# Storing the last dwq and dwo blocks from GpSimd's queue, two partitions and then 126

## The chip, the cores and the metric

The kernel runs on one core of one Trainium2 chip. The metric is device time of one execution in microseconds; the median of several runs is compared. Beside it there is one profiled execution, whose page and trace are quoted below. In the trace, times count from the span's start; "SPq" and "POOLq" are the instruction queues of SyncE and GpSimd, and DMA queue q1 carries what SyncE issues, q0 what GpSimd issues.

## The reference

Forward and backward pass of a gated mix of two branches, for one token (batch 1, sequence 1, D = 640), with ten outputs: the result and nine gradients.

```python
x = A_x
g = _sigmoid((x * gate_w).sum(-1, keepdims=True))
a = _A_ref(x, A_k_cache, A_v_cache, A_wq, A_wo)   # q = x@wq; softmax(q k^T) v; @wo; 32 heads, 4096 keys, Dh 128
b = _B_ref(x, B_w1, B_b1, B_w2)                   # mish(x@w1 + b1) @ w2; F = 1728
return g * a + (1 - g) * b
...
_out, _vjp = jax.vjp(_f, A_x, A_k_cache, A_v_cache, A_wq, A_wo, B_w1, B_b1, B_w2, gate_w)
_grads = _vjp(grad_out)
```

All arrays are bf16. The K and V caches are 32 MB each, and so are their gradients. The gradients of wq (640 x 4096) and wo (4096 x 640) are outer products: dwq is x times the gradient of q, dwo is the attention output o times the gradient that comes in.

## The kernel before

The loop runs over the 32 heads `h`, in 8 groups `g` of 4. For each head it loads K and V (1 MB each, `load_k`, `load_v`), transposes them on TensorE, forms the softmax and its gradient, and builds the gradients of K and V as outer products on VectorE (`dk_out`, `dv_out`, through `out_half`, L598), each stored with one transfer of 1 MB from SyncE's queue (L616). All heavy loads and stores are issued by SyncE, in the order in which they are written out by hand in the loop; an issue waits on SyncE until its data are ready, and holds up the issues behind it.

The weights come in blocks. A tile `wq_p` (128 partitions x 5 x 1024 bf16, 1.25 MB) holds wq of two groups; a tile `wo_g` (128 x 4 x 640 bf16, 640 KB) holds wo of one. When a group is done, `f_dwq` and `f_dwo` write the gradients over the weights in the same tiles, and `f_dwq_st` (L377) and `f_dwo_st` (L386) store them. In DRAM, a partition's piece of dwq is five runs of 2048 bytes that lie far apart; its piece of dwo is one run of 5120 bytes.

After the loop stands a tail for the last head and the last group. In it the gradient of the last K block is stored (L616), then come dwq (`f_dwq` on VectorE, `l_dwq` on ScalarE for the last head) with its store, dwo (`l_dwo` on VectorE, L383) with its store, and a short chain that ends in `fin_rows`, 15 rows of 256 bytes, which GpSimd stores in three transfers of five rows (L920 to L922). GpSimd's queue is otherwise hardly used: it has memsets at the start, a few small transfers and two multiplications; between L802 and L920 it stands waiting.

```python
    dk_out(h, 1)
    ...
    for c in range(RC):
        l_dwq(c, 3, 4)
    f_dwq_st(g)
    for t in range(G):
        l_dwo(t)
    f_dwo_st(g)
    l_add(g, NG, True)
```

Of the kernel before, what the change touches and what calls it, by code (L numbers as in the profile page):

```python
# [16 lines left out]
def kernel(  # L17
# [24 lines left out]
    nc = tc.nc  # L42
    P = 128
    _, H, Sk, Dh = A_k_cache.shape
    D = A_x.shape[-1]
# [4 lines left out]
    G = 4  # L50
    NG = H // G
    GD = G * Dh
# [17 lines left out]
    dwq_v = out_4.rearrange("(rc r) c -> r rc c", r=P)  # L70
    wo4_v = A_wo.rearrange("(g p t) n -> g p t n", p=P, t=4)
    dwo4_v = out_5.rearrange("(g p t) n -> g p t n", p=P, t=4)
# [29 lines left out]
    kts, vts, wqs, wos = {}, {}, {}, {}  # L102
# [11 lines left out]
    wqp = {}  # L114
# [255 lines left out]
    def f_dwq(g, c, a=0, b=G):  # L370
        cs = slice(a * Dh, b * Dh)
        nc.vector.tensor_scalar(wqs[g][:, c, cs], groups[g]["dq_bc"][:, cs], x_col_f[:, c:c + 1], None, ALU.mult)  # L372

    def f_dwq_st(g):
        for k, (a, z) in enumerate(WQP):
            if g == z - 1:
                nc.sync.dma_start(dwq_v[:, :, a * GD:z * GD], wqp[k][:])  # L377

    def f_dwo(g, hh):
        nc.scalar.activation(wos[g][:, hh, :], da_bc[:], ACT.Copy, scale=groups[g]["o4"][:, hh:hh + 1])  # L380
# [2 lines left out]
        nc.vector.tensor_scalar(wos[NG - 1][:, hh, :], da_bc[:], groups[NG - 1]["o4"][:, hh:hh + 1], None, ALU.mult)  # L383

    def f_dwo_st(g):
        nc.sync.dma_start(dwo4_v[g], wos[g][:])  # L386

    h_sb = const.tile([P, FCN], F32, name="h_sb")
    u_sb = const.tile([P, FCN], F32, name="u_sb")
# [353 lines left out]
    for h in range(H - 1):  # L743
        g, hh = h // G, h % G
# [65 lines left out]
        if hh == 0:  # L810
            if nx:
                g_new(g + 1)
            if pv:
                l_pe(g - 1, 0, G)
                l_add(g - 1, g - 1, True)
                for t in range(G):
                    f_dwo(g - 1, t)
                f_dwo_st(g - 1)
                for c in range(2):
                    f_dx(g - 1, c)  # L820
                    f_dwq(g - 1, c)
        if hh == 1:
            if pv:
                for c in range(2, RC):
                    f_dx(g - 1, c)
                    f_dwq(g - 1, c)
                f_dwq_st(g - 1)
            if nx:
                w_pe("o", g + 1, 0)
                ev()  # L830
                w_pe("o", g + 1, 1)
                ev()
# [22 lines left out]
    g, h = NG - 1, H - 1  # L855
# [34 lines left out]
# [7 lines that stand above are left out]
    fin = const.tile([P, 3 * RC], F32, name="fin")  # L897
# [55 lines left out]
```

## Time and profile before

| | |
|---|---|
| median of 3 runs | 404.82 us (404.8 to 405.51) |
| the profiled execution | 404.96 us |
| its span, first to last instruction | 403.2 us |
| PE, DVE, ACT, POOL busy | 76%, 71%, 58%, 3% of the span |
| DMA | 164.55 MB, 408 GB/s over the span |
| q1 (SyncE) | 28256 packets, 163.97 MB |
| q0 (GpSimd) | 384 packets, 0.10 MB |

The page divides the span into 40 slices; in nearly all of them the DMA engines are busy at nine tenths or more. The time of an execution is the span and 1.76 us around it. The trace keeps the single DMA packets (queue, size, start, duration) and the semaphore updates of the transfers, sixteen for a transfer, one for each DMA engine, but not which engine sent which.

### The profile page before, as it was taken

To read this page: it belongs to the slowest core of one execution; us is meant where nothing else is said; L and a number is where in the kernel's file an instruction comes from. 1 tells how busy PE (TensorE), PEld (TensorE's weight loads), DVE (VectorE), ACT (ScalarE), POOL (GpSimd) and SP (SyncE) were. 2 spreads that over 40 slices of the span, in tenths; PEclk is the share of its full clock that TensorE was granted. 3 is DMA by queue.
4 is the path that set the end of the run, shared out by engine and by line. 5 is a ranking of instruction groups with operands and counts; after the bars stand their busy time and mean duration, and the time that the engine had idled before them with its cause. 6 is when DMAs were issued, how large, how long until landed. Compare 5 with 4: busy or idle time off the path is not lost.

```text
span 403.2 us, 7688 instructions
## 1 busy us (share of the span) xinstructions
PE 305.9 (76%) x2930; PEld 207.0 (51%) x2945; DVE 287.9 (71%) x808; ACT 232.4 (58%) x468; POOL 11.8 (3%) x29
## 2 busy tenths in 40 slices
PE   2979989787897985876887779876886977677640
PEld 1556646464565663544555447544555645464420
DVE  2217738868678875769897956896997985679780
ACT  2466757754676563753668667765767655375220
POOL 3000001000000000000001200000000000000001
PEclk9999999988999998989998997988999899889555
DMA  7999999999999999999999999999999999999894
GB/s 274 428 416 423 417 424 415 417 423 424 422 422 426 423 414 424 424 418 428 422 423 428 424 418 424 427 418 423 422 419 424 425 417 425 426 422 377 360 389 153
DMA packets 28708, 164.55 MB, mean 408 GB/s; under 512 B 2991, under 2 KB 3056, under 8 KB 12288
## 3 DMA queue, kind: packets, MB, share of 16 engines
q1 hardware_dynamic: 28256, 163.97, 98.1%
q8 instruction: 23, 0.38, 0.4%
q0 software_dynamic: 384, 0.10, 0.1%
q14 instruction: 13, 0.11, 0.1%
q10 hardware_dynamic: 32, 0.01, 0.0%
HBM read 82.03 MB, written 82.03 MB: 407 GB/s over the span
## 4 chain that ended last, share of the span: by engine, by line
DMA 42%; PE 25%; DVE 22%; ACT 6%; issue 2%; POOL 0%; POOLq 0%; SPq 0%; DVEq 0%; ACTq 0%
DMA out_dram<-o_sb 40%; PE tr L515 9%; DVE o_sb L598 9%; PE rw L538 3%; PE rw L631 3%; DVE junk L362 3%; DMA wq_p<-in_A_wq_dram 2%; PE x L555 2%; DVE wq_p L372 2%; ACT rw_sb L549 2%; ACT do_row L266 2%; PE tr L324 2%; PE do_ps L263 1%; PE h_ps L405 1%; DVE mjunk L494 1%
## 5 line engine op out<-in xcount | busy, mean ns | idle before, releaser
L524 ACT COPY T<-tr 128x512 f32<-128x512 f32 x256 | 138.0, 595 | 53.0 <-PE tr L515 38.3
L598 DVE TENSOR_TENSOR o_sb<-qs_row,ds 128x2048 bf16<-128x2048 bf16 x58 | 70.8, 1220 | 37.6 <-DMA out_dram<-o_sb 37.5
L515 PE MATMUL tr<-ident_f,Kn 128*128 128x128 f32 x512 | 85.6, 295 | 5.8 <-DVE rw L508 5.8
L515 PE MATMUL tr<-ident_f,Vn 128*128 128x128 f32 x512 | 84.5, 299 | 6.6 <-ACT T L524 6.0
L515 PEld LDWEIGHTS tr<-ident_f,Vn 128*128 128x128 f32 x512 | 63.4, 154 | 27.3 <-PE tr L515 12.1
L515 PEld LDWEIGHTS tr<-ident_f,Kn 128*128 128x128 f32 x512 | 61.1, 149 | 23.2 <-PE rw L631 14.1
L598 DVE TENSOR_TENSOR o_sb<-do_row,p 128x2048 bf16<-128x2048 bf16 x58 | 68.2, 1218 | 0.0
L549 ACT COPY rw_sb<-rw 128x512 f32<-128x512 f32 x33 | 19.4, 587 | 51.2 <-PE rw L538 49.0
L631 PE MATMUL rw<-Kn,ds 128*4 128x512 bf16 x256 | 35.9, 405 | 6.4 <-DVE ds L593 5.7
L631 PE MATMUL rw<-Vn,p 128*4 128x512 bf16 x256 | 35.9, 405 | 0.0
L567 PE MATMUL mx<-ident_f,m_s 128*128 128x128 f32 x32 | 10.1, 316 | 29.7 <-DVE m_s L563 29.6
L555 PE MATMUL x<-ident_f,rw_sb 128*128 128x128 f32 x132 | 22.5, 295 | 4.4 <-ACT rw_sb L549 1.4
L362 DVE SCALAR_TENSOR_TENSOR junk<-wq_p,dq_bc 128x512 bf16<-128x512 bf16 x35 | 23.9, 684 | 0.0
L538 PE MATMUL rw<-T,qz 128*32 128x512 bf16 x256 | 22.3, 426 | 0.0
L575 ACT ACTIVATE e_bf<-x,negM 128x32 bf16<-128x32 f32 x32 | 9.3, 292 | 22.4 <-DVE dqo L639 22.1
L567 PEld LDWEIGHTS mx<-ident_f,m_s 128*128 128x128 f32 x32 | 4.5, 142 | 34.0 <-DVE m_s L563 33.9
L538 PE MATMUL rw<-T,doz 128*32 128x512 bf16 x256 | 21.4, 411 | 0.8 <-ACT T L524 0.8
L380 ACT ACTIVATE wo_g<-da_bc,o 128x640 bf16<-128x640 bf16 x28 | 20.9, 816 | 1.2 <-PE ax_ps L350 1.2
L583 PE MATMUL mx<-zd,ones_f 128*128 128x2 f32 x64 | 11.2, 245 | 13.5 <-DVE pj L579 13.4
L555 PEld LDWEIGHTS x<-ident_f,rw_sb 128*128 128x128 f32 x132 | 14.5, 145 | 13.2 <-ACT rw_sb L549 13.2
L569 DVE TENSOR_REDUCE negM<-mx 128x1 f32<-128x128 f32 x32 | 9.2, 288 | 16.1 <-PE mx L567 16.1
L631 PEld LDWEIGHTS <-ds 128*4 128x4 bf16 x256 | 9.1, 85 | 22.2 <-DVE ds L593 11.4
(174 smaller groups left out, 367.6 us busy)
## 6 DMA issues: line engine op xcount, KB each, us to landing
out_dram<-o_sb SPq DMA_DIRECT2D x58, 1024.0 KB, 16.6
Kn<-in_A_k_cache_dram SPq DMA_DIRECT2D x32, 1024.0 KB, 16.8
Vn<-in_A_v_cache_dram SPq DMA_DIRECT2D x32, 1024.0 KB, 17.3
wq_p<-in_A_wq_dram SPq DMA_DIRECT2D x4, 1280.0 KB, 8.7
wo_g<-in_A_wo_dram SPq DMA_DIRECT2D x8, 640.0 KB, 17.6
out_dram<-wo_g SPq DMA_DIRECT2D x8, 640.0 KB, 18.3
out_dram<-wq_p SPq DMA_DIRECT2D x4, 1280.0 KB, 16.3
out_dram<-Kn SPq DMA_DIRECT2D x3, 1024.0 KB, 11.4
```

Source lines behind the costliest of these rows:

```text
L362: nc.vector.scalar_tensor_tensor(jq[:], in0=wqs[g][:, c, :], scalar=1.0, in1=groups[g]["dq_bc"][:], op0=ALU.mult, op1=ALU.mult, accum_out= ...
L380: nc.scalar.activation(wos[g][:, hh, :], da_bc[:], ACT.Copy, scale=groups[g]["o4"][:, hh:hh + 1])
L515: nc.tensor.transpose(tp[:, t, :], words[:, t * P:(t + 1) * P], ident_f[:])
L524: nc.scalar.copy(T[h][:, (3 - c) * (TB // 2):(4 - c) * (TB // 2), :], tp[:])
L538: nc.tensor.matmul(rw[32 * c:32 * (c + 1), :], lhsT=z[:, par, :, :].rearrange("p m u -> p (m u)"), rhs=Tb[:, c, par, :, :], start=first an ...
L549: nc.scalar.copy(rw_sb[h][:].rearrange("p t r -> p (t r)"), rw[:])
L555: nc.tensor.transpose(xs[h][:, 3 - j, :], t[:, j, :], ident_f[:])
L567: nc.tensor.transpose(mx[:, 0:P], dgms.pop(h)[:].to_broadcast([P, P]), ident_f[:])
L575: nc.scalar.activation(es[h][:], sd[h][0], ACT.Exp, bias=negM[:], scale=scale, accum_out=zds[h][:, 0:1])
L583: nc.tensor.matmul(mx[:, P:P + 2], lhsT=ones_f[:], rhs=zds[h][:], start=True, stop=True)
L598: nc.vector.tensor_tensor(dst[:, a:b, :].rearrange("p j (k t) -> p j k t", t=4), row.rearrange("p (k t) -> p k t", t=4).unsqueeze(1).to_br ...
L631: nc.tensor.matmul(rw[32 * c:32 * c + 4, :], lhsT=c4[:, 4 * jb:4 * jb + 16].rearrange("p (j t) -> p t j", t=4)[:, 0, :], rhs=N[:, jb:jb + ...
```

## The change

The last group's two stores are issued by GpSimd in place of SyncE, each as two transfers: partitions 0 and 1, and partitions 2 to 127. Of dwo, a partition's run of 5120 bytes is cut in two of 2560 (the argument is a limit in bytes), so that it has two strides as dwq has. The stores of the other groups are as before.

```diff
+    def st_parts(dst, src, run):
+        for a, b in ((0, 2), (2, P)):
+            nc.gpsimd.dma_start(dst[a:b], src[a:b], max_dma_last_dim=run)
+
     def f_dwq_st(g):
         for k, (a, z) in enumerate(WQP):
             if g == z - 1:
-                nc.sync.dma_start(dwq_v[:, :, a * GD:z * GD], wqp[k][:])
+                if g == NG - 1:
+                    st_parts(dwq_v[:, :, a * GD:z * GD], wqp[k][:], 2 * (z - a) * GD)
+                else:
+                    nc.sync.dma_start(dwq_v[:, :, a * GD:z * GD], wqp[k][:])
...
     def f_dwo_st(g):
-        nc.sync.dma_start(dwo4_v[g], wos[g][:])
+        if g == NG - 1:
+            st_parts(dwo4_v[g], wos[g][:], 2 * G * D // 2)
+        else:
+            nc.sync.dma_start(dwo4_v[g], wos[g][:])
```

In the built program the four transfers stand on GpSimd's queue ahead of the three of `fin_rows`: 2 x 5 x 1024 elements (waiting for ScalarE's last product), 126 x 5 x 1024, 2 x 2 x 1280 (waiting for VectorE's last product), 126 x 2 x 1280. No other instruction changes its place.

## The prediction

> **What bounds the kernel now.** I read the end of the span first, because only the last two stores change. The chain of waits ends with GpSimd's last issue, near 395.2 us, so eight microseconds at the end belong to no engine's work. The stretches of the end show what fills them (columns: busy time of each engine, granted clock, DMA share, GB/s):
>
> ```profile
> 396.00:398.00 2.00, 0.00 (x0) 0.00 (x0) 0.00 (x0) 0.00 (x0) 0.00 (x0) 0.50 0.37 133
> 398.00:400.00 2.00, 0.00 (x0) 0.00 (x0) 0.00 (x0) 0.00 (x0) 0.00 (x0) 0.50 0.07 26
> 400.00:402.00 2.00, 0.00 (x0) 0.00 (x0) 0.00 (x0) 0.00 (x0) 0.00 (x0) 0.50 0.05 23
> ```
>
> A share of 0.07 is one DMA engine of sixteen (0.0625), and 2048 bytes every 80 ns, as its packets stand in the trace, is 25.6 GB/s. For the last four microseconds one engine alone sends. SyncE's waits name what it sends:
>
> ```profile
> SPq L948 <- DMA out_dram<-wo_g: 1.5, 1, 1.5
> SPq L948 <- DMA out_dram<-Kn: 1.2, 1, 1.2
> SPq L948 <- DMA out_dram<-wq_p: 1.0, 1, 1.0
> ```
>
> The issues stand in the timeline of SyncE and GpSimd:
>
> ```profile
> 388.13 0.33 SPq L616 DMA_DIRECT2D out_dram<-o_sb  x1
> 389.58 0.38 SPq L377 DMA_DIRECT2D out_dram<-wq_p  x1
> 390.73 0.39 SPq L386 DMA_DIRECT2D out_dram<-wo_g  x1
> 393.67 0.53 POOL L920 DMA_DIRECT2D out_dram<-fin_rows  x1 [100.69 <-ACT fin_rows L919]
> 394.70 0.50 POOL L922 DMA_DIRECT2D out_dram<-fin_rows  x1
> ```
>
> Each transfer has sixteen landings in the trace. The middle one, the last but one and the last are: K gradient (L616) 391.9, 393.2, 397.5; dwq (L377) 395.3, 396.3, 400.6; dwo (L386) 397.0, 397.8, 402.2. So fourteen engines are done at 397.0, one is 0.8 late, one 5.1, and the span ends 1.02 us after the late one (402.16 to 403.18). The lag is old: it is 1.0 us near 95, 4.0 near 204, 8.1 near 361. Beside it the page has an instruction queue, q8, with 23 packets of 16 KB of about 1 us each, spread over the run; I take it (an inference) that they pass through the late engine.
>
> **What the change removes.** From SyncE's queue two issues; nothing stands behind them there but the end. From the late engine's q1 queue its share of both stores: 40 packets of 2048 bytes at 80 ns (3.2 us) and 8 of 5120 at 193 ns (1.54 us). Its K share still ends near 397.0 and lands at 397.5, so whatever else is done, the span can't end before 397.5 + 1.02 = 398.5.
>
> **How the new shares fall.** This is the step that decides. In the trace a transfer of 128 or 64 rows uses sixteen engines with equal shares (the 64 rows of L800 are 16 packets of 5120 bytes, four rows each), and the five-row ones of `fin_rows` have five data packets each. I assume that a transfer with two strides is dealt out in equal shares over as many engines, up to sixteen, as divide its rows: two rows over two engines, 126 over fourteen, nine rows each, and that the second starts where the first stopped. Then two engines have one row and fourteen have nine, in both stores. [...]
>
> Is the late engine one of the two? On it, the packets of all three `fin_rows` transfers hold data (256-byte packets at 397.99, 398.49, 398.99), while the engine that is 0.8 late has none in all three. So five rows go to the same five engines each time, and the late one is among them. If rows are dealt from the first engine on, it is one of the first five; the two rows of the change go to the first two. Equal weights would give 2 in 5. An engine that alone serves an instruction queue is more likely the first or second of a numbering than the fifth, so I put 0.6.
>
> **The sum, if it is.** GpSimd's issue costs, from its timeline:
>
> ```profile
> 1.27 0.72 POOL L155 DMA_DIRECT2D b_sb<-in_B_b_dram  x1 [0.82 <-DVE b_sb L154]
> 291.88 0.57 POOL L800 DMA_DIRECT2D out_dram<-w_sb  x1 [68.10 <-ACT w_sb L503]
> ```
>
> These have 128 and 64 runs; five runs took 0.50 to 0.53. From 5 to 128 that is (0.72 - 0.51) / 123 = 1.7 ns a run on 0.5 us. The two-row transfer of dwq is issued at about 389.6, as L377 was, and takes 0.53. The large one has 630 runs: 0.5 + 1.07 = 1.57 us, to 391.7. The small one of dwo takes 0.5, the large one (252 runs) 0.93, to 393.1; `fin_rows` is ready at 393.4, so nothing on GpSimd is held up. SyncE's place was free 1.2 us earlier, but no data wait for it.
>
> From the start of an issue to the first packet, L920 needed 2.92 us and the others 3.7 to 4.4, with the DMA engines full. The fourteen engines finish K at about 391.6 and then stand empty, so L920 is nearest. First packet of the large dwq piece: 390.13 + 2.92 + 1.07 = 394.1. The gap of 2.5 us is new; before, dwq lay queued behind K. Then 45 packets at 80 ns, 3.6 us, and 18 of 2560 bytes at about 0.10 us (between 84 ns for 2048 and 135 ns for 3456), 1.8 us: 399.5. Landing 0.40 later, as before (401.76 to 402.16), and 1.02 to the end: 400.9 for the span. The late engine has its K share, one row of each store (0.6 us) and a landing at about 398.1, below that. `fin_rows` stands behind the same shares in q0 and lands with them. The span falls from 403.2 to 400.9, by 2.3 us; the profiled execution lies 0.14 above the median, so 404.82 - 2.3 = **402.5**.
>
> Ends of this sum: with no cost per run, and the first packet 2.92 after the issue, 3.3 us of gain, 401.5; over half of the gain goes if the first packet needs 1.3 more, as L155's did: 403.8.
>
> [...]
>
> **Rivals.** (1) *The light share falls on other engines.* The late engine then takes nine rows in place of eight: 0.40 us for dwq, 1.80 - 1.54 = 0.26 for dwo. It is backlogged until 397, so the late start costs it nothing. 405.5, and up to 405.9 if `fin_rows` behind the shares costs it 0.1 to 0.4 more (its three landings there are 0.48 apart). For it: three of the first five engines; a lucky start of the dealing is not shown. Chance 0.22.
>
> (2) *The pieces spread over all sixteen engines anyway*, so no load moves, and the change does not do what it says: at eight rows each (126 rounded up) the late engine keeps eight or has one more. 404.8 to 405.5. For it: five rows went to fixed engines, with no sign of a rotation. Against: those have one stride, these two. Chance 0.13. [...]
>
> (3) *GpSimd takes too long over the 896 runs*, and it becomes the bound: slower. The 1.7 ns a run may not be all; part may lie hidden between issue and first packet. L155, with 128 runs, needed 4.18 there and L920, with five, 2.92: if runs make the difference, 10 ns a run. With p ns a run, the large dwq piece's packets end at 396.6 + 0.63 p and the last at 1.8 more; that equals the 401.76 of before at p = 5.3. At 10 ns it ends at 404.7, three late: 407.8. Against: L410, with at most 32 runs, needed 4.3. Chance 0.15.
>
> **How the numbers follow.** What a measurement of this kernel can tell from no change is about 0.2%, 0.8 us. The forecast, with the shares as assumed and the late engine light, has 0.50 (0.60 for the late engine, less the parts of rivals 2 and 3); nearly all of it is faster by more than 0.8, 0.47, and 0.03 same. Rival 1 lies at the bound: 0.08 same, 0.14 slower. Rival 2: 0.07 and 0.06. Rival 3: 0.01 and 0.14. Together 0.47 faster, 0.19 same, 0.34 slower. The likeliest case alone spans 401.5 to 403.8. The range goes a little below it and takes in rivals 1 and 2 and the cheap half of rival 3: 401.2 to 406.0.
>
> **What would show it.** If right, the last two microseconds of the span no longer have one engine at 25 GB/s; q0 carries 1.97 MB; the landings of the four pieces lie within 0.5 us of each other but for the one-row engines; and the fourteen engines have a gap of about 2.5 us after 391.8. If rival 1 or 2 holds, the tail at 24 GB/s stays, now on q0. If rival 3 holds, POOL's two large issues take over 3.5 and 1.5 us, and the DMA share is low between 392 and 397. The step most likely to be wrong is which engines get the single rows; the second is the time from issue to first packet.

## The result: slower by half a percent

Five runs of the changed kernel have a median of 407.36 us (406.1 to 407.79), against 404.82 before (404.67 to 405.51): a ratio of 1.0056, with a 95% interval of 1.0038 to 1.0075. It was forecast faster, at 402.5, and the result lies above the range. The profiled execution took 407.27 us, with a span of 405.50 (403.18 before).

The stretches of the end, after the change (columns as before: busy time of the engines, granted clock, DMA share, GB/s):

```profile
392.00:394.00 2.00, 0.28 (x1) 0.09 (x1) 0.21 (x2) 0.26 (x1) 1.54 (x3) 0.50 0.99 292
394.00:396.00 2.00, 0.00 (x0) 0.00 (x0) 0.00 (x0) 0.00 (x0) 0.74 (x2) 0.50 0.90 310
396.00:398.00 2.00, 0.00 (x0) 0.00 (x0) 0.00 (x0) 0.00 (x0) 0.00 (x0) 0.50 0.81 280
398.00:400.00 2.00, 0.00 (x0) 0.00 (x0) 0.00 (x0) 0.00 (x0) 0.00 (x0) 0.50 0.28 91
400.00:402.00 2.00, 0.00 (x0) 0.00 (x0) 0.00 (x0) 0.00 (x0) 0.00 (x0) 0.50 0.09 34
402.00:404.00 2.00, 0.00 (x0) 0.00 (x0) 0.00 (x0) 0.00 (x0) 0.00 (x0) 0.50 0.03 13
```

The two stretches of the kernel before from 392 to 396:

```profile
392.00:394.00 2.00, 0.28 (x1) 0.09 (x1) 0.69 (x4) 0.26 (x1) 0.33 (x1) 0.50 1.02 385
394.00:396.00 2.00, 0.00 (x0) 0.00 (x0) 0.00 (x0) 0.00 (x0) 1.20 (x3) 0.50 1.07 414
```

Two things stand in these lines. The tail of one engine is still there (0.09, then 0.03, where one engine is 0.06), now on q0. And between 392 and 396 the engines are nearly as busy as before, 0.99 and 0.90 against 1.02 and 1.07, but move 292 and 310 GB/s against 385 and 414: for the same busy time they move a tenth to a fifth less, so packets take longer.

GpSimd's issues, in its timeline, and the DMA view of the end (q0's packets, MB and share of the sixteen engines from 390 to 406, then transfers with the median time to landing):

```profile
389.71 1.62 POOL L376 DMA_DIRECT2D out_dram<-wq_p  x2 [97.24 <-ACT wq_p L367]
391.33 1.38 POOL L376 DMA_DIRECT2D out_dram<-wo_g  x2
393.16 0.55 POOL L930 DMA_DIRECT2D out_dram<-fin_rows  x1 [0.46 <-ACT fin_rows L929]
```

```profile
q0 software_dynamic: 736, 1.97, 38.1%
...
out_dram<-wq_p POOLq DMA_DIRECT2D x1, 1260.0 KB, 11.2
out_dram<-wo_g POOLq DMA_DIRECT2D x1, 630.0 KB, 11.5
out_dram<-fin_rows POOLq DMA_DIRECT2D x3, 1.2 KB, 10.1
out_dram<-wq_p POOLq DMA_DIRECT2D x1, 20.0 KB, 5.4
```

GpSimd is quick: 1.62 us for the two pieces of dwq, 1.38 for the two of dwo, `fin_rows` not held up. What SyncE waits for at the end is one name now:

```profile
SPq L958 <- DMA out_dram<-fin_rows: 16.1, 1, 16.1
```

In the sixteen landings of the large dwq piece, two come at 392.9 and 393.2, nine between 396.2 and 396.8, four up to 399.1, and one at 401.5; of the large dwo piece two at 395.4 and 395.7, the middle ones at 398, the last at 403.45; of the last `fin_rows` transfer the last at 404.02. By the dealing as assumed, the two early engines are the same in both. So the shares fell as assumed, two engines with one row and fourteen with nine; but the late engine, whose K share landed at 398.1, was not one of the two.

### The profile page after: what moved, and what is told of

Same layout as the page of the kernel before. It is cut to its first block, busy times and chain, and to the rows that moved or that the text cites. A ratio compares the mean times of both kernels' runs of the same rounds, so it can differ in the third digit from the quotient of the medians.

```text
span 405.5 us, 7690 instructions
## 1 busy us (share of the span) xinstructions
PE 303.8 (75%) x2930; PEld 205.9 (51%) x2945; DVE 287.8 (71%) x808; ACT 232.8 (57%) x468; POOL 14.9 (4%) x33
## 3 DMA queue, kind: packets, MB, share of 16 engines
q0 software_dynamic: 1024, 2.07, 1.6%
## 4 chain that ended last, share of the span: by engine, by line
DMA 46%; DVE 23%; PE 21%; ACT 5%; issue 2%; POOL 0%; POOLq 0%; SPq 0%; DVEq 0%; ACTq 0%
DMA out_dram<-o_sb 44%; DVE o_sb L608 8%; PE tr L525 8%; DVE junk L362 3%; PE rw L548 3%; PE rw L641 2%; DMA wq_p<-in_A_wq_dram 2%; DVE wq_p L372 2%; PE x L565 2%; PE tr L324 1%; PE q_ps L211 1%; ACT do_row L266 1%; ACT rw_sb L559 1%; PE do_ps L263 1%; PE h_ps L415 1%
## 5 line engine op out<-in xcount | busy, mean ns | idle before, releaser
L525 PE MATMUL tr<-ident_f,Kn 128*128 128x128 f32 x512 | 84.2, 291 | 5.6 <-DMA Kn<-in_A_k_cache_dram 5.6
L641 PE MATMUL rw<-Kn,ds 128*4 128x512 bf16 x256 | 34.8, 395 | 6.5 <-DVE ds L603 5.9
L641 PE MATMUL rw<-Vn,p 128*4 128x512 bf16 x256 | 34.8, 395 | 0.0
```

The costliest lines, as they stand in the source:

```text
L525: nc.tensor.transpose(tp[:, t, :], words[:, t * P:(t + 1) * P], ident_f[:])
L641: nc.tensor.matmul(rw[32 * c:32 * c + 4, :], lhsT=c4[:, 4 * jb:4 * jb + 16].rearrange("p (j t) -> p t j", t=4)[:, 0, :], rhs=N[:, jb:jb + ...
```

## What the late engine did

The last landing of a large transfer is taken as the late engine's (for the last K gradient it comes 4 us or more behind the last but one), so its work can be followed through the end. The clock starts at its landing of the K gradient of head 30. From there it sends a V and a K share (eight packets of 8192 bytes, one every 306 ns, 2.45 us for each share), then its rows of dwq (before: 40 packets, one every 80 ns) and dwo (0.193 us a row). On q0 the rows of dwq travel in packets of 4096 bytes, one every 155 ns (each lasts 159), which is nearly the same speed. "Nominal" is the sum of these for the rows it has in the kernel; "over" is what the trace shows beyond it, to the landing of its last large share.

| kernel | its rows of dwq, dwo | starts at | large shares landed | nominal | over | small landings behind | to the end of the span |
|---|---|---|---|---|---|---|---|
| before | 8, 8 | 392.46 | 402.16 | 9.64 | 0.06 | none | 1.02 |
| the change | 9, 9 | 391.98 | 403.45 | 10.14 | 1.33 | 0.57 | 1.48 |
| one transfer each (e3) | 8, 8 | 392.25 | 401.81 | 9.54 | 0.02 | 0.58 | 1.40 |
| 112 and 16 rows (e5) | 8, 8 | 392.44 | 404.10 | 9.54 | 2.12 | 0.76 | 1.49 |
| light by shift (e2) | 1, 1 | 392.82 | 401.04 | 5.48 | 2.74 | 1.33 | 1.56 |
| only dwo, first pair light (e10) | 8, 9 | 392.65 | 402.52 | 9.84 | 0.03 | none | 1.08 |
| only dwo, late engine light (e7) | 8, 1 | 392.99 | 401.41 | 8.29 | 0.13 | none | 1.08 |

The change against before: it started 0.48 earlier, had 0.50 more to send, lost 1.27 to slow packets, 0.57 to small transfers queued behind and 0.46 between last landing and end: 2.32 in all, which is the difference of the spans. (The 0.57 is the three `fin_rows` transfers, each landing 0.19 behind the one before.) Each row stands on one profiled execution; that of e5 is the slowest of its six (408.17, median 407.61).

## Experiments

Two theories at first. **A**: shares are dealt as assumed and the late engine got nine rows. **B**: GpSimd's queue itself costs, wherever the shares fall. A third, **C**, came out of the first runs: an engine that sends other rows than it would in a transfer of 128 slows its neighbours' packets.

### Moving the light pair (e1, e2)

A load with two strides of n rows into a scratch tile goes ahead at the start of the kernel, and one of 16 - n behind the pieces, so that, if each transfer is dealt on from where the one before stopped, the dealing has moved on by n when the stores come and is back where it began at the end. e1 has n = 2, e2 n = 3.

```diff
+    step_sb = const.tile([16, 2, 4], BF16, name="step_sb")
+    def step(a, b):
+        nc.gpsimd.dma_start(step_sb[a:b, :, 0:2], B_w1[a:b, 0:8].rearrange("p (s t) -> p s t", s=2)[:, :, 0:2])
+    step(0, n)
...
     f_dwo_st(g)
+    step(n, 16)
```

> The four pieces as in the change, but a load of 2 rows with two strides into a scratch tile goes ahead on GpSimd's queue at the start of the kernel, and one of 14 rows behind the pieces, so that the dealing should have moved on by two engines when the pieces are issued. Theory A (shares of 1 and 9 rows are dealt as assumed, but the late engine is the third, fourth or fifth and got nine rows): if it is the third or fourth, it is light now; the stretch in which one engine sends alone goes, and the time falls to 405 to 405.8, no longer bound by the late engine but by the slower ones among the other fourteen (which landed up to 401.4 with the change). If it is the fifth: 407.4 as with the change. Theory B (GpSimd's queue itself is what costs, in landing and at the end of the program, wherever the shares fall): 407.4.

> As the run before with 3 rows ahead and 13 behind: the light pair should be the fourth and fifth engine. Theory A: late engine third: 407.4, one engine alone at the end; fourth or fifth: 405 to 405.8. Together with the run before this names the engine. Theory B: 407.4.

e1: 408.25 us, ratio 1.0087 (1.0074 to 1.0100), above the 407.4 that it was given, with the late engine's dwo share last at 403.85. e2: 405.94, ratio 1.0029 (1.0017 to 1.0041). So the late engine is neither in the first pair nor the second, but in the pair after a shift by three: it is the fifth. That fits what the prediction read from `fin_rows` (one of the five), and theory A. But e2 missed the gain that a light late engine should bring, and its trace shows why:

```profile
394.00:396.00 2.00, 0.00 (x0) 0.00 (x0) 0.00 (x0) 0.00 (x0) 0.12 (x1) 0.50 0.96 334
396.00:398.00 2.00, 0.00 (x0) 0.00 (x0) 0.00 (x0) 0.00 (x0) 0.00 (x0) 0.50 0.88 260
398.00:400.00 2.00, 0.00 (x0) 0.00 (x0) 0.00 (x0) 0.00 (x0) 0.00 (x0) 0.50 0.23 61
400.00:402.00 2.00, 0.00 (x0) 0.00 (x0) 0.00 (x0) 0.00 (x0) 0.00 (x0) 0.50 0.06 15
```

Busy at 0.96 with 334 GB/s, then 0.88 with 260. In the packets, the late engine's last 8192-byte ones, the K share that it had to itself, took 1304, 1060, 991, 392 and 495 ns in place of 309. It was slowed not by its own load but by what the others did, and its K share landed at 401.0 (397.5 before). Behind it came seven more landings 0.19 apart, of transfers of which this engine had one row of data or none.

### Queue or shares (e3, e4)

```diff
 # e3: one transfer of 128 partitions each, from GpSimd
-        for a, b in ((0, 2), (2, P)):
+        for a, b in ((0, P),):
 # e4: the pieces of the change, from SyncE
-            nc.gpsimd.dma_start(dst[a:b], src[a:b], max_dma_last_dim=run)
+            nc.sync.dma_start(dst[a:b], src[a:b], max_dma_last_dim=run)
```

> Both stores from GpSimd's queue in one transfer of 128 partitions each, so that every engine has eight rows. Theory A: the late engine has 0.66 us less to send than with the change and its packets are not slowed by others (with the change, 1.4 us of slower packets); what is left over the kernel before is the later landing (0.86 us after the last packet in place of 0.40) and the later end (1.48 after the last landing in place of 1.02): 405.4 to 406. Theory B: 406.8 to 407.4, like the change.

> The same four pieces, but issued by SyncE. Theory A: the uneven shares cost on this queue too. If SyncE deals each piece from the first engine on, the first two engines have ten rows, the last two none, and the late one nine: 0.66 us more and slower packets, 405.5 to 407. Theory B: the queue was the cost, so 404.8 to 405.5.

e3: 405.71, ratio 1.0020 (1.0012 to 1.0029). e4: 407.91, ratio 1.0078 (1.0064 to 1.0091). Theory B falls: the queue without uneven shares costs 0.8 us, and uneven shares without the queue cost 3.0, more than the change and more than theory A gave them (405.5 to 407). The DMA view of e3 from 390 to 406, and the stretches of e4:

```profile
q0 software_dynamic: 576, 1.97, 32.5%
```

```profile
402.00:404.00 2.00, 0.00 (x0) 0.00 (x0) 0.00 (x0) 0.00 (x0) 0.00 (x0) 0.50 0.07 26
404.00:406.00 2.00, 0.00 (x0) 0.00 (x0) 0.00 (x0) 0.00 (x0) 0.00 (x0) 0.50 0.07 26
```

The same 1.97 MB kept the engines busy for 32.5% of 16 us, 5.2 us each on average, where the change needed 38.1%, 6.1 us. That is the slow packets in one number. Packet by packet: of the 4096-byte packets of q0 a fifth (0.205) took over 1.3 times their 159 ns with the change, none with e3. This fraction is called the slow share below. In e4 the late engine alone sends until 406; its last share landed at 406.37, some 3 us later than its packets need at their usual spacing. (That profile is the slowest of e4's six executions, 409.06.)

### What makes packets slow (e5, e8, e9)

```diff
 # e5: sixteen engines, seven rows and one, no load moved
+        for a, b in ((0, 112), (112, P)):
 # e9: partitions 0 to 63, 64 to 127
+        for a, b in ((0, 64), (64, P)):
 # e8: dwq as 8 and 120 rows, dwo in one transfer; step(0, 13) ahead, step(0, 12) behind
+                    st_parts(dwq_v[:, :, a * GD:z * GD], wqp[k][:], 2 * (z - a) * GD, ((0, 8), (8, P)))
```

> Each of the two stores from GpSimd as 112 rows and 16 rows: sixteen engines with seven and one, so eight each and no load moved. It tells what the slow packets of the change hang on (a fifth of its 4096-byte packets took over 1.3 times 159 ns, none did in one transfer of 128 rows). Theory C, an engine that sends other rows than it does in a transfer of 128 gets in the way of its neighbours: slow share 0.1 to 0.3 again, 406.3 to 407.2. Theory D, the slow packets come from nine rows on fourteen engines or from two queues on the late engine: share near 0, 405.7 to 406.1, as with one transfer plus the two more issues.

e5: 407.61, ratio 1.0067 (1.0053 to 1.0080), slow share 0.35: theory C. Every engine has eight rows here, in pieces that sixteen divides, and it is as slow as the change. The rival D, that nine rows on fourteen engines or the second queue make them slow, falls. The late engine lost 2.1 us. The time is above what C was given.

> dwq as 8 rows and 120 rows, shifted so that fifteen engines have eight rows each in a block (rows 8 to 15, 16 to 23 and so on) and the late one a single row; dwo in one transfer of 128 from GpSimd. [...]

> Both stores from GpSimd, each as partitions 0 to 63 and 64 to 127, no step: eight rows of each for every engine, four and four. [...] If slow packets come only from engines that have drifted apart: share 0.1 to 0.35 as in the change and with 112 and 16, 405.7 to 407.

e8: 406.38, ratio 1.0039 (1.0025 to 1.0053), slow share 0.57. e9: 405.79, ratio 1.0023 (1.0014 to 1.0032), slow share 0.65, half of the packets at 320 ns or more. DMA view from 390 to 406, of e5, e8 and e9 in turn:

```profile
q0 software_dynamic: 624, 1.97, 43.4%
```

```profile
q0 software_dynamic: 672, 1.97, 47.8%
```

```profile
q0 software_dynamic: 608, 1.97, 47.4%
```

For e8 a slow share over 0.5 had been estimated ahead of the run, for e9 one over 0.6, and both came: 0.57 and 0.65, the second far above the 0.1 to 0.35 that was given to slow packets from engines that have drifted apart alone. What the estimates took as the cause, engines that get in each other's way by the rows that they read at the same time, was the author's guess and is not shown. What was measured is the slow share by the way in which dwq is dealt: 0.65 as 64 and 64 rows (e9, half of the packets at twice their time), 0.57 as 8 and 120 (e8), 0.35 as 112 and 16 (e5), 0.205 as 2 and 126 (the change), none as 128 in one transfer (e3). In e9 none of the 5120-byte packets of dwo was slow (all near 196 ns). (A piece of dwo is short there, four rows and 0.78 us an engine; that this is the reason is not shown.) Whether the reads or the writes into DRAM slow the packets was not separated.

e9 shows, too, what slow packets cost: its other fifteen engines ended dwo between 397.4 and 401.7, most of them 2 to 4 us later than in e3 (396.2 to 397.4), and yet its time is that of e3 (405.79 against 405.71), under the 406 to 408 that had been estimated with the late engine slowed as well, because the late engine's 8192-byte packets were not slowed (none over 1.3 times) and it ended at 402.7, against 402.4. In these runs slow packets cost only where they hit the engine that ends last, or make another one the last.

### Moving less (e6, e7, e10, e11, e12)

Only one of the two stores goes by pieces; the other is SyncE's as before. e6, e7 and e11 shift by three (late engine light), e10 does not.

```diff
 # e7 (with step(0, 3), step(3, 16)) and e10 (without): dwq as in the kernel before
-                if g == NG - 1:
-                    st_parts(dwq_v[:, :, a * GD:z * GD], wqp[k][:], 2 * (z - a) * GD)
-                else:
-                    nc.sync.dma_start(dwq_v[:, :, a * GD:z * GD], wqp[k][:])
+                nc.sync.dma_start(dwq_v[:, :, a * GD:z * GD], wqp[k][:])
 # e6: the same for dwo; e12: e7 without step(3, 16)
 # e11: e7, and dwq in four fifths by SyncE and the last in two pieces by GpSimd
```

> Dealing shifted by three, so that the late engine (the fifth) is light, but for dwq alone; dwo goes by SyncE in one transfer as in the kernel before. The late engine sends K, dwo and one row of dwq, 3.2 - 0.4 = 2.8 us less than before. Theory C: its packets are slowed while the others send dwq (the K share took 3.7 us longer in the run with both shifted), so gain and loss nearly cancel: 404.5 to 406. Theory D, or no slowing: 402.5 to 404.

> The same for dwo alone; dwq goes by SyncE in one transfer. The late engine sends 1.54 - 0.2 = 1.3 us less than before; the others send uneven shares for under 2 us only, so less slowing: theory C: 404.3 to 405.5 (1.3 less, then some 0.5 to 1 for slow packets and about 0.8 that the way over GpSimd cost in one transfer). Theory D: 403.8 to 404.6.

> The change for dwo alone, not shifted, so that the first two engines are light and the late one (the fifth) has nine rows; dwq by SyncE in one transfer. Against the run with dwo alone shifted by three (404.23) it differs only in who is light. If that is what decides: the late engine sends 1.8 us in place of 0.2, and the three small transfers land behind it: 405.5 to 406.3. If it does not matter who is light: 404 to 404.5.

e6: 405.14, ratio 1.0009 (1.0001 to 1.0018): gain and loss cancel, as C said; the late engine lost 1.1 us to slow packets. They were packets of dwo, which SyncE sent whole here: 0.27 of all its 5120-byte packets took over 1.3 times 196 ns, so a transfer of 128 is slowed, too, while another is under way in pieces. e7: 404.23, ratio 0.9987 (0.9979 to 0.9996), just under what C was given (D's range, 403.8 to 404.6, held it, but e5 had ruled D out). e10: 405.11, ratio 1.0004 (0.9995 to 1.0013), lower than expected: `fin_rows` did not land behind the late engine's last share, since dwq on q1 ended later (402.52) than all of q0 (399.97). e7 and e10 differ in who is light (and in the two small loads): 0.9 us between the medians, 0.8 when each is taken against the kernel before of its own session. In e7's end the tail is shorter:

```profile
398.00:400.00 2.00, 0.00 (x0) 0.00 (x0) 0.00 (x0) 0.00 (x0) 0.00 (x0) 0.50 0.09 28
400.00:402.00 2.00, 0.00 (x0) 0.00 (x0) 0.00 (x0) 0.00 (x0) 0.00 (x0) 0.50 0.03 12
402.00:404.00 2.00, 0.00 (x0) 0.00 (x0) 0.00 (x0) 0.00 (x0) 0.00 (x0) 0.50 0.00 0
```

One engine still sends alone at 400, but it stops near 401; it sends dwq, and nothing of the others lands after 399.8.

> dwo light for the late engine as before (404.23), and the last fifth of dwq, too; the other four fifths by SyncE. The late engine sends 0.64 - 0.1 us less. If its dwq landing (401.4, the others at 399.8) is what ended that run: 403.7 to 404.1. If slow packets or two more issues take it back: 404.2 to 405.

> The fastest version (dwo light for the late engine, dealing shifted by three at the start, 404.23) without the load of 13 rows at the end that brings the dealing round to where it began. It tells whether the place in the dealing outlives an execution. If every execution begins at the first engine: 404.0 to 404.4 with little spread, since only an issue of 0.5 us and a landing of 0.2 are gone and neither ended the span. If the place carries over: each execution's light pair lies three engines further on, the late engine is light in one of eight, and the median is like the run with the first pair light, 405.1, with single runs down to 404.2.

e11: 404.56, ratio 0.9991 (0.9980 to 1.0002); more of the load moved brings no more. e12: 404.14, ratio 0.9988 (0.9979 to 0.9997), single runs from 403.86 to 405.0. If the place in the dealing carried over, the median would be e10's. So every execution begins at the same engine, as far as these runs tell, and the load at the end is not needed. e7 and e12 are the two versions that beat the kernel before, by about 0.5 us.

## Why the prediction was wrong

**What bounds the end**: right. One late engine ends the span, before and after, and the experiments' times follow from when that engine is done and what lands behind it. e8 seems to be the exception: there the late engine's K share landed at 398.85 with 1.54 us of dwo to send, but the last share of dwo landed at 402.58.

**The cost of GpSimd's issues**: right, and rival 3 is out. Of the 1.62 us for the two pieces of dwq, the small one took 0.64 and the large one, from 390.34, took 0.99 for 630 runs: 0.8 ns a run beyond 0.5 us, where 1.7 were taken. The first packet of the large piece stood in the trace at 391.9, some 1.6 us after that start and not 3.99 as in the sum: the gap on the fourteen engines that was to cost 2.5 us was about 0.9 (their last K packets end near 391.05, their first of dwq start near 392.0).

**How the shares fall**: right in sizes and rotation, and rival 2 is out. The rows of dwq are 640 runs of 2048 bytes; q0 carried them as 312 packets of 4096 bytes and 16 of 2048, which fits 22 and one on each of fourteen engines (nine rows of five runs) and two and one on each of two (one row). That the next piece starts where the last ended fits e1 and e2: one row more sent ahead (408.25 us with two, 405.94 with three) made the late engine light.

**Who is light**: wrong; this is the step that failed. The late engine had been narrowed to five by the `fin_rows` packets; 2 in 5 was what the trace gave, and 0.6 was put on an argument from numbering that no row bore out. It is the fifth. Rival 1 was the case. The chances did not follow from that 0.6 either: less rivals 2 and 3 it leaves 0.43 for the forecast and 0.29 for rival 1, where 0.50 and 0.22 were written.

**The rival's price**: mis-sized. It had 405.5 to 405.9; measured 407.36. Its extra rows were right (0.66 there, 0.50 by the packets of q0). `fin_rows` behind the shares cost 0.57, where 0.1 to 0.4 had been allowed, and the span ends 1.48 after a last landing on q0, not 1.02. Missing altogether is the largest term, 1.3 us of slow packets on the late engine: every packet was given the duration of its row in the trace of before, where rows are dealt eight to an engine as in a transfer of 128. The nearest row to another dealing, the 64 rows of L800, is one packet to an engine (196 to 219 ns), too short to show it. The slow packets would have sunk the forecast even with the right pair, as e2 shows (405.94, with two small loads more).

**GpSimd's issues beside VectorE**: VectorE's products for dwo ran from 388.93 to 390.19, GpSimd began at 389.71, beside them, and had issued both pieces of dwq by 391.33. No hold shows, though the overlap is only 0.5 us. Nor did one in the kernel before: L800, with 64 runs, issued at 291.88 beside a product of VectorE (291.74 to 292.96), took 0.57 us; L410, with at most 32, issued at 56.86 with VectorE idle, 0.51.

## What to carry to other kernels

When a span ends in a DMA tail, count the landings engine by engine: a tail at a sixteenth of the DMA share (0.07 with 26 GB/s in the kernel before) is one engine, and the two versions here that were clearly faster (e7, ratio 0.9987, and e12, 0.9988) both moved load off that engine. How a transfer's rows are dealt to engines is a cost of its own: dwq had no slow packets where both stores went as 128 partitions in one transfer (the kernel before, e3) and a slow share of 0.205 to 0.65 where it went in pieces (the change, e5, e8, e9), and versions with both stores split by partitions were 1.0 to 3.4 us slower than the kernel before, where the whole transfers from GpSimd cost 0.8. Move the smallest, last share, check in the trace which engine it left, and keep small transfers out of the queue behind it (three of them cost 0.57 us behind the change's last share).

## What was not expected of the hardware

- The same 1.97 MB kept the DMA engines busy for 32.5% of 16 us when dealt as 128 rows, 38.1% as 2 and 126, 43.4% as 112 and 16, and 47.4% as 64 and 64.
- A slowed engine's 8192-byte packets took up to 1304 ns in place of 309. The busy share hides it: from 396 to 398, where that packet falls, it was 0.88 with 260 GB/s.
- Transfers that follow each other on GpSimd's queue land 0.19 us apart on the late engine, even where it has no data of theirs: seven of them added 1.33 us in e2.
- After a last landing of a transfer of GpSimd's queue the span went on for 1.40 to 1.57 us, after one of SyncE's for 0.91 to 1.08.

Why one engine is late was not tried; that it carries the instruction queue stays an inference.
